# Attention and two mixtures on one core: gates turned by TensorE, next tokens ahead of next weights, rows of the second dense chunk six units later

## The chip, the cores and the metric

The kernel runs on one core of one Trainium2 chip. The metric is the device time of one execution in microseconds (us), lower being better. TensorE does the matmuls (its weight loads are listed apart), VectorE, ScalarE and GpSimd the elementwise work, and SP issues most of the DMAs.

## The reference, cut to what matters

Three stages follow one another; all inputs and the output are float32.

```python
# attention with decay: q, k, v are (4, 8, 576, 64), f is (4, 8, 576)
cum = cumsum(log(clip(f, 1e-4, 1)), -1)
attn = softmax(causal(q @ k^T / 8 + cum[..., :, None] - cum[..., None, :]))
x = heads_side_by_side(attn @ v)                    # 2304 tokens x 512
# one of 8 experts per token (w1: 512 x 1024, w2: 1024 x 512)
logits = unit(x) @ unit(expert_emb).T / tau
e = argmax(logits); gate = softmax(logits)[e]
x = gate * (relu(x @ w1[e]) @ w2[e])
# dense layer for all tokens (w_in: 512 x 2048, w_out: 2048 x 512)
out = softplus(x @ w_in) @ w_out
```

## The kernel before

Every float32 matrix is split into a high part, rounded to the matmul's format, and a low part, the rest; three matmuls (high by high, high by low, low by high) stand for one. ScalarE makes the high part and VectorE (sometimes GpSimd) the low part.

**Attention** (up to about 230 us) computes the 32 heads in pairs and writes the tokens to `xd` in DRAM. **Routing** (`route`, to about 255 us) finds which tokens go to which expert and gives the gather and scatter indices. The change touches neither.

**Experts** (`experts`, L900, about 256 to 545 us) runs nine phases in the order of `ORDER` (L41), each one expert's weights with a block of its tokens: phases 0, 5, 7 and 8 are of kind "t" (three rows of 128 tokens), phases 1 to 4 of kind "b" (two rows), phase 6 of kind "s" (one row). `wide` (L1020) computes the first two kinds, `small` (L1067) the last.

A wide phase has two layers. The first computes eight blocks of 128 hidden features from the turned tokens `xh`, `xl` and the four weight pieces 0 to 3 (`wh`, `wl`; L1037), and ScalarE and VectorE turn each block into `hh`, `hl`. The second (`l2`, L1011, matmuls at L1017) runs over the eight blocks, a unit each: 6 matmuls of 512 columns with two rows, 9 with three, 3 with one. Then `scatter` sends the rows to their places in `yd`.

Between these, the loops issue the work for the next phase:

- `feed` (L964) calls `wsplit` (L943): SP loads one piece of 512 KB into a buffer `raw`, ScalarE writes `wh` (L957), VectorE `wl` (L958). Pieces 4 to 7 of the phase's own second layer come during its first layer, pieces 0 to 3 of the next phase during its second layer. The pool of `raw` has four buffers, which the format conversions of the dense weights (`conv.step`, L1208) share; the table `STEPS` (L38) says at which units those run. A load can start when the VectorE work of the piece four before it has ended.
- `xprep(ph + 1)` (L982) turns the next phase's tokens: for each row four TensorE transposes into a PSUM bank (L994; the pool has two banks), `xh` on ScalarE (L995), `xl` on VectorE (L996). `xgather(ph + 2)` (L972) then gathers the tokens after those through GpSimd's queue.

Each engine executes its instructions in the order in which these calls issue them.

**Gates.** `gates` (L845) is called after phase 0. It computes the gate of every token as `gs`, 128 partitions by 20 columns, five columns for each of the four batches of 576 tokens (four of 128 tokens, one of 64). The dense layer wants `gate` with 18 columns of 128 consecutive tokens. Before, GpSimd's queue writes `gs` to DRAM (`gd`, eight DMAs, L860 and L861) and reads it back (L862), in runs of 4 bytes.

**Dense layer** (`ffn`, L1236, from about 550 us). The 18 rows of 128 tokens form chunks of 4, 3, 4, 3 and 4 rows (`SIZES`); each has 16 units `fb`. A unit's step issues `l1` (12 matmuls, L1293), the softplus on ScalarE, GpSimd (`e`, L1306) and VectorE (result `gh`, `gl`), and the second layer `l2` of the unit three before (L1335). In units 1 to 6 of the first chunk GpSimd also makes the low part of one piece of `w_out` each (L1229). A row of the next chunk is loaded (`yload`, L1260), scaled by its gate on GpSimd and a unit later turned by TensorE and split (`yprep`, L1269); these calls stand at the end of a unit:

```python
for a in range(SIZES[c + 1]):
    if fb == 3 * a:
        yload(c + 1, a)
    if fb == 1 + 3 * a:
        turn = yprep(c + 1, a)
        next(turn)
    if fb == 2 + 3 * a:
        next(turn, None)
```

Of the kernel before, what the change touches and what calls it, by code (L numbers as in the profile page):

```python
# [9 lines left out]
F32 = mybir.dt.float32  # L10
# [14 lines left out]
B, H, S, D = 4, 8, 576, 64  # L25
N = B * S
# [5 lines left out]
T = 5 * B  # L32
# [15 lines left out]
@with_exitstack  # L48
def body(ctx, tc, q, k, v, f, emb, tau, w1, w2, win, wout, out):
    nc = tc.nc  # L50
    const = ctx.enter_context(tc.tile_pool(name="const", bufs=1))
    dram = ctx.enter_context(tc.tile_pool(name="dram", bufs=1, space=DRAM))
    stage = ctx.enter_context(tc.tile_pool(name="stage", bufs=4))
    g = Shared()
    g.stage = stage
    g.xd = dram.tile([N, DM], F32, name="xd")
    g.yd = nc.dram_tensor("yd", [N + 128 * NSLOT, DM], F32, kind="Internal").ap()
    g.ydv = dram_disjoint_views(g.yd, NSLOT)
    g.gd = dram.tile([N, 1], F32, name="gd")
    g.ncum = dram.tile([B * H, S], F32, name="ncum")  # L60

    nc.scalar.preload_act_table_set(LN_EXP)
    g.ident = const.tile([128, 128], F32, name="ident")
    make_identity(nc, g.ident)
    g.gidx = const.tile([128, NMAIN], I32, name="gidx")
    g.sidx = const.tile([128, NMAIN], I32, name="sidx")
    g.ids = const.tile([1, 3 * NG + 4], I32, name="ids")
    g.gate = const.tile([128, N // 128], F32, name="gate")
    g.lt = const.tile([128, T, E], F32, name="lt")
    g.mx = const.tile([128, T, 1], F32, name="mx")  # L70
    g.nrm = const.tile([128, T], F32, name="nrm")
    g.gs = const.tile([128, T], F32, name="gs")
    g.nr = const.tile([128, T, 1], F32, name="nr")

    g.const = const
    g.pre = []
    with ExitStack() as acc:
        ps_s = attention(tc, g, acc, q, k, v, f, emb, tau, w1)
        g.home = ctx.enter_context(tc.tile_pool(name="home", bufs=17, reuse_waits="tile"))
        ring = ctx.enter_context(tc.tile_pool(name="ring", bufs=8, reuse_waits="tile"))  # L80

        def wtile(dt=F32R):
            return (ring.tile([128, 1024], dt, name="wh", tag="wh"), ring.tile([128, 1024], dt, name="wl", tag="wl"))

        g.wtile = wtile
        g.w2a = w2[0]
        with ExitStack() as rtx:
            route(tc, g, rtx.enter_context(tc.tile_pool(name="r_p", bufs=1)), ps_s)
    experts(tc, g, w1, w2, win, wout, out)


# [753 lines left out]
def gates(tc, g):  # L845
    nc = tc.nc
    V = nc.vector
    lt, nr, gs = g.lt, g.nr, g.gs
    nc.scalar.activation(nr[:, :, 0], g.nrm, ACTF.Sqrt)
    nc.scalar.preload_act_table_set(LN_EXP)  # L850
    V.tensor_scalar(nr, nr, 1e-6, None, op0=ALU.add)
    V.reciprocal(nr, nr)
    V.tensor_tensor(lt, lt, g.mx.to_broadcast([128, T, E]), op=ALU.subtract)
    V.tensor_tensor(lt, lt, nr.to_broadcast([128, T, E]), op=ALU.mult)
    nc.scalar.activation(lt, lt, ACTF.Exp)
    V.tensor_reduce(gs, lt, op=ALU.add, axis=AX.X)
    V.tensor_scalar(gs, gs, 1e-9, None, op0=ALU.add)
    V.reciprocal(gs, gs)
    for b in range(B):
        nc.gpsimd.dma_start(g.gd[b * S:b * S + 512, :].rearrange("(r p) o -> p (r o)", p=128), gs[:, 5 * b:5 * b + 4])  # L860
        nc.gpsimd.dma_start(g.gd[b * S + 512:b * S + S, :], gs[0:64, 5 * b + 4:5 * b + 5])  # L861
    nc.gpsimd.dma_start(g.gate, g.gd.rearrange("(t p) o -> p (t o)", p=128))  # L862


def tail_slots(tc, g, p, psp, scratch, M):
# [34 lines left out]
def experts(tc, g, w1, w2, win, wout, out):  # L900
# [6 lines left out]
    with ExitStack() as ctx:  # L907
# [112 lines left out]
        def wide(ph):  # L1020
# [30 lines left out]
            for i, (rows, fb) in enumerate([([a], fb) for a in range(w) for fb in range(8)] if last else  # L1051
                                           [(list(range(w)), fb) for fb in range(8)]):
                l2(ph, py, hts[fb], fb, rows)
                if i == 2:
                    xprep(ph + 1)
                    xgather(ph + 2)
                if not last:
                    feed(ph, min(i + 1, 4))
                if not last and STEPS[ph][8 + i]:
                    conv.step()  # L1060
                if last and i % 3 == 1:
# [5 lines left out]
        def small(ph, after1=None):  # L1067
# [48 lines left out]
            py = [ps_y.tile([128, DM], F32, name="y", tag="y")]  # L1116
            for fb in range(8):
                l2(ph, py, hts[fb], fb, [0])
                if fb == 1 and not after1:
                    hts += turn(h1)  # L1120
                if fb == 3 and main:
                    xprep(ph + 1)
                    xgather(ph + 2)
                if fb < 4:
                    next_weights(fb + 1)
            scatter(ph, 0, py[0])
# [54 lines left out]
        xgather(1)  # L1181
        for c in range(4, 8):
            wsplit(0, c)
        for ph in range(n_ph):
            (small if phases[ph][0] == "s" else wide)(ph)
            W.pop(ph)
# [49 lines left out]
def ffn(tc, g, conv, out):  # L1236
# [6 lines left out]
    with ExitStack() as ctx:  # L1243
# [111 lines left out]
        for n in range(len(units) + 3):  # L1355
# [15 lines left out]
            if n >= 3:  # L1371
                l2(*units[n - 3])
            if n < len(units) and c + 1 < NC:
                for a in range(SIZES[c + 1]):
                    if fb == 3 * a:
                        yload(c + 1, a)
                    if fb == 1 + 3 * a:
                        turn = yprep(c + 1, a)
                        next(turn)
                    if fb == 2 + 3 * a:  # L1380
                        next(turn, None)


# [33 lines left out]
```

## Time and profile before

| | |
|---|---|
| three runs | 983.41, 978.90 and 975.82 us, median 978.9 |
| profiled execution | 976.53 us, of which the span from first to last instruction is 974.4 |
| mean granted clock of TensorE | 0.963 of full speed |
| busy | TensorE 889.7 us, its weight loads 760.5, VectorE 616.5, ScalarE 604.3, GpSimd 352.5 |

Rows of the trace give a start in us from the beginning of the span, a duration in us, the engine, the line, the operation, what it writes and reads, and in square brackets the idle time before it with the instruction or DMA that ended it. PE is TensorE, DVE VectorE, ACT ScalarE, POOL GpSimd, SPq the DMA issues of SP. A row may stand for several instructions (x2). Ends of matmuls are modelled, so the distance of starts is the better measure of them.

### The profile page before, as it was taken

To read this page: it belongs to the slowest core of one execution; us is meant where nothing else is said; L and a number is where in the kernel's file an instruction comes from. 1 tells how busy PE (TensorE), PEld (TensorE's weight loads), DVE (VectorE), ACT (ScalarE), POOL (GpSimd) and SP (SyncE) were. 2 spreads that over 40 slices of the span, in tenths; PEclk is the share of its full clock that TensorE was granted. 3 is DMA by queue.
4 is the path that set the end of the run, shared out by engine and by line. 5 is a ranking of instruction groups with operands and counts; after the bars stand their busy time and mean duration, and the time that the engine had idled before them with its cause. 6 is when DMAs were issued, how large, how long until landed. Compare 5 with 4: busy or idle time off the path is not lost. (4 is left out here: it accounts for less than half of the span.)

```text
span 974.4 us, 17371 instructions
## 1 busy us (share of the span) xinstructions
PE 889.7 (91%) x6292; PEld 760.5 (78%) x6292; DVE 616.5 (63%) x1321; ACT 604.3 (62%) x1139; POOL 352.5 (36%) x479
## 2 busy tenths in 40 slices
PE   3999999998199599899899579999999999999998
PEld 2788887887199489797788468889988888998886
DVE  3888888887676367666669547455546455555444
ACT  4778888786525255544435367667677666767664
POOL 6776786773403112111101047223323222322221
PEclk9999999999599889999899789999999999999999
DMA  8766665741537887777764200001001001000001
GB/s 182 170 156 150 159 162 141 209 105 37 209 102 195 143 282 271 268 239 246 246 222 162 89 12 12 11 1 66 23 1 54 11 1 54 23 1 33 1 0 44
DMA packets 103327, 109.41 MB, mean 112 GB/s; under 512 B 62584, under 2 KB 71800, under 8 KB 103232
## 3 DMA queue, kind: packets, MB, share of 16 engines
q1 hardware_dynamic: 99296, 97.02, 35.4%
q0 software_dynamic: 3680, 11.03, 3.3%
q8 instruction: 51, 0.84, 0.4%
q14 instruction: 44, 0.36, 0.1%
q10 hardware_dynamic: 256, 0.16, 0.1%
HBM read 93.16 MB, written 15.03 MB: 111 GB/s over the span
## 5 line engine op out<-in xcount | busy, mean ns | idle before, releaser
L1323 DVE TENSOR_TENSOR gl<-e,gh 128x512 fp32r<-128x512 f32 (+1 forms) x80 | 99.2, 1239 | 178.0 <-ACT gh L1321 178.0
L1306 POOL TENSOR_TENSOR e<-u,e 128x512 f32<-128x512 f32 (+1 forms) x80 | 94.6, 1182 | 291.4 <-ACT u L1305 271.4
L1293 PE MATMUL h<-yth,dl 128*128 128x512 f32 (+1 forms) x320 | 119.0, 372 | 0.0
L1302 ACT ACTIVATE e<-h 128x512 f32<-128x512 f32 (+1 forms) x80 | 44.4, 556 | 113.5 <-PE h L1293 94.8
L1335 PE MATMUL o<-dl,gh 128*128 128x512 f32 x288 | 112.5, 391 | 0.0
L958 DVE TENSOR_TENSOR wl<-raw,wh 128x1024 fp32r<-128x1024 f32 x64 | 77.7, 1223 | 33.3 <-ACT wh L957 32.7
L957 ACT ACTIVATE wh<-raw 128x1024 fp32r<-128x1024 f32 x64 | 66.7, 1056 | 38.0 <-DMA raw<-in_moe_w_dram 37.3
L1037 PE MATMUL h<-xh,wh 128*128 128x384 f32 (+1 forms) x256 | 81.7, 319 | 8.4 <-ACT xh L995 6.9
L1037 PE MATMUL h<-xl,wh 128*128 128x384 f32 (+1 forms) x256 | 81.1, 317 | 2.7 <-DVE xl L996 2.7
L1037 PE MATMUL h<-xh,wl 128*128 128x384 f32 (+1 forms) x256 | 80.8, 316 | 0.5 <-issue 0.5
L320 DVE SCALAR_TENSOR_TENSOR pts<-pt,pts 128x512 f16<-128x512 f32 (+3 forms) x128 | 69.8, 567 | 11.9 <-ACT pts L317 11.2
L317 ACT ACTIVATE pts<-pt 128x512 f16<-128x512 f32 (+3 forms) x128 | 58.4, 495 | 22.1 <-PE pt L330 10.6
L294 ACT ACTIVATE p<-sm,mx 128x512 f32<-128x512 f32 (+3 forms) x128 | 67.8, 558 | 0.0
L1017 PE MATMUL y<-wh,hh 128*128 128x512 f32 x168 | 67.5, 402 | 0.0
L1017 PE MATMUL y<-wl,hh 128*128 128x512 f32 x168 | 66.4, 395 | 0.8 <-DVE wl L958 0.8
L1293 PEld LDWEIGHTS h<-yth,dl 128*128 128x128 f32 x320 | 60.8, 190 | 7.8
L291 DVE CUSTOM_DVE_ANT_0 sm<-s,cb 128x512 f32<-128x512 f32 (+3 forms) x128 | 58.3, 484 | 8.0 <-PE s L271 7.1
L1008 POOL DMA_INDIRECT yd<-y,sidx x21 | 21.2, 1007 | 115.9 <-ACT y L1001 112.9
L978 POOL DMA_INDIRECT xg<-xd,gidx x21 | 24.6, 1169 | 105.7 <-PE xt L994 95.8
L1318 DVE TENSOR_TENSOR e<-e,v 128x512 f32<-128x512 f32 (+1 forms) x80 | 57.5, 718 | 7.7 <-DVE e L1317 0.5
L1335 PEld LDWEIGHTS o<-dl,gh 128*128 128x128 f32 x288 | 54.1, 188 | 10.3
L1293 PE MATMUL h<-yth,wh 128*128 128x512 f32 (+1 forms) x160 | 61.5, 384 | 0.7 <-ACT yth L1281 0.7
(294 smaller groups left out, 2606.2 us busy)
## 6 DMA issues: line engine op xcount, KB each, us to landing
raw<-in_moe_w_dram SPq DMA_DIRECT2D x68, 512.0 KB, 4.5
cb<-ncum SPq DMA_DIRECT2D x32, 288.0 KB, 4.8
raw<-in_moe_w_in_dram SPq DMA_DIRECT2D x16, 512.0 KB, 5.7
raw<-in_moe_w_out_dram SPq DMA_DIRECT2D x16, 512.0 KB, 3.9
cb<-ncum SPq DMA_DIRECT2D x32, 144.0 KB, 4.5
out_dram<-ob SPq DMA_DIRECT2D x18, 256.0 KB, 2.4
qt<-in_q_dram SPq DMA_DIRECT2D x32, 128.0 KB, 2.6
kt<-in_k_dram SPq DMA_DIRECT2D x32, 128.0 KB, 2.5
```

The lines of the kernel that those rows point to most:

```text
L291: nc.vector.tensor_tensor_reduce(out=s[:, 0:n], in0=ps[h][:, 0:n], in1=c[:, h, 0:n], scale=-0.125, scalar=1e30, op0=ALU.add, op1=ALU.min, ...
L294: nc.scalar.activation(p[:, 0:n], s[:, 0:n], ACTF.Exp, scale=-1.0, bias=m)
L317: nc.scalar.activation(hi, ps, ACTF.Copy, scale=UP)
L320: nc.vector.scalar_tensor_tensor(lo, ps, UP, hi, op0=ALU.mult, op1=ALU.subtract)
L957: nc.scalar.activation(hi, r, ACTF.Copy)
L958: nc.vector.tensor_sub(lo, r, hi.bitcast(F32))
L1017: nc.tensor.matmul(py[a], x[:, 128 * a:128 * a + 128], w[:, fb % 2], start=(fb == 0 and m == 0 and w is wh), stop=(fb == 7 and m == 1))
L1037: nc.tensor.matmul(pl, x[:, fs], y[:, c], start=(c == 0 and m == 0), stop=(c == 3 and m == 2))
L1293: nc.tensor.matmul(pl, w[:, fs], x[:, d], start=(d == 0 and m == 0), stop=(d == 3 and m == 2))
L1306: nc.gpsimd.tensor_sub(e, u, e)
L1323: nc.vector.tensor_sub(gl, d, gh.bitcast(F32))
L1335: nc.tensor.matmul(PO[c][a], x, w, start=(fb == 0 and m == 0 and w is wh), stop=(fb == FB - 1 and m == 1))
```

## The change

Three edits. The gates are turned on the core: a first transpose gives 20 x 128, VectorE swaps its two halves of 64, a second transpose turns it back, and four copies put the pieces in place. The two transposes stand after units 5 and 6 of phase 1's second layer. In a phase's second layer, `xprep` and `xgather` come after the first unit (before: after the third in `wide`, the fourth in `small`), and in `wide` the pieces of the next weights come one unit later; in `small` the turn of the second hidden half comes after the first unit too (before: the second). In the dense layer, the three rows of the second chunk are loaded and turned in units 6 to 14 of the first, before in 0 to 8.

```diff
-    for b in range(B):
-        nc.gpsimd.dma_start(g.gd[b * S:b * S + 512, :].rearrange("(r p) o -> p (r o)", p=128), gs[:, 5 * b:5 * b + 4])
-        nc.gpsimd.dma_start(g.gd[b * S + 512:b * S + S, :], gs[0:64, 5 * b + 4:5 * b + 5])
-    nc.gpsimd.dma_start(g.gate, g.gd.rearrange("(t p) o -> p (t o)", p=128))
+def turn_gates(tc, g, p, psp):
+    nc = tc.nc
+    V = nc.vector
+    t = psp.tile([128, 128], F32, name="gt", tag="T")
+    nc.tensor.transpose(t[0:T], g.gs, g.ident)
+    turned = p.tile([T, 2, 64], F32, name="turned", bufs=1)
+    for x in range(2):
+        V.tensor_copy(turned[:, x], t[0:T, 64 - 64 * x:128 - 64 * x])
+    yield
+    t = psp.tile([128, 128], F32, name="gt", tag="T")
+    nc.tensor.transpose(t[:, 0:T], turned.rearrange("p x n -> p (x n)"), g.ident[0:T, 0:T])
+    to = g.gate.rearrange("p (b t) -> p b t", b=2)
+    here = g.gs.rearrange("p (b x t) -> p b x t", b=2, x=2)[:, :, 0]
+    there = t[:, 0:T].rearrange("p (b x t) -> p b x t", b=2, x=2)[:, :, 1]
+    V.tensor_copy(to[:, :, 0:4], here[:, :, 0:4])
+    V.tensor_copy(to[0:64, :, 4:5], here[0:64, :, 4:5])
+    V.tensor_copy(to[64:128, :, 4:9], there[64:128])
+    V.tensor_copy(to[0:64, :, 5:9], there[0:64, :, 0:4])
...
@@ wide
-                if i == 2:
+                if i == 0:
                     xprep(ph + 1)
                     xgather(ph + 2)
-                if not last:
-                    feed(ph, min(i + 1, 4))
+                elif not last:
+                    feed(ph, min(i, 4))
+                if ph == 1 and i in (5, 6):
+                    next(turned, None)
                 if not last and STEPS[ph][8 + i]:
                     conv.step()
...
@@ small
-                if fb == 1 and not after1:
+                if fb == 0 and not after1:
                     hts += turn(h1)
-                if fb == 3 and main:
-                    xprep(ph + 1)
-                    xgather(ph + 2)
+                    if main:
+                        xprep(ph + 1)
+                        xgather(ph + 2)
...
@@ ffn
+                x = 0 if c else 6
                 for a in range(SIZES[c + 1]):
-                    if fb == 3 * a:
+                    if fb == x + 3 * a:
                         yload(c + 1, a)
...
```

Three places of the order show what moves. First VectorE in phase 1, from the end of its first layer to the first block of phase 2; `wl` are weight splits, `xl` the next tokens, `dw` a format conversion, `hl` the phase's hidden features. Before:

```order
L958 TENSOR_TENSOR wl<-raw,wh 128x1024 x3
L1220 TENSOR_SCALAR dw<-raw 128x512
L1221 SCALAR_TENSOR_TENSOR dw<-raw,dw 128x512
L1222 SCALAR_TENSOR_TENSOR dw<-raw,dw 128x512
L996 TENSOR_TENSOR xl<-xt,xh 128x4x128 x2
L958 TENSOR_TENSOR wl<-raw,wh 128x1024 x2
L1043 SCALAR_TENSOR_TENSOR hl<-h,hh 128x512
```

The same place now, with `turned` and `gate` as the copies of the gates:

```order
L973 TENSOR_TENSOR wl<-raw,wh 128x1024
L1011 TENSOR_TENSOR xl<-xt,xh 128x4x128 x2
L973 TENSOR_TENSOR wl<-raw,wh 128x1024
L1238 TENSOR_SCALAR dw<-raw 128x512
L1239 SCALAR_TENSOR_TENSOR dw<-raw,dw 128x512
L1240 SCALAR_TENSOR_TENSOR dw<-raw,dw 128x512
L973 TENSOR_TENSOR wl<-raw,wh 128x1024 x3
L867 COPY turned<-gt 20x64 x2
L874 COPY gate<-gs 128x2x4
L875 COPY gate<-gs 64x2
L876 COPY gate<-gt 64x2x5
L877 COPY gate<-gt 64x2x4
```

The two `xl` moved from behind the first two pieces of the next weights to ahead of them, the conversion from behind the second piece to ahead of it, and the six copies stand behind all four pieces.

Next ScalarE in phase 6, the small one; `hs` are its hidden features before the turn, `hh<-ht` after it, `xh` the tokens of phase 7. Before:

```order
L1079 ACTIVATE hs<-h 128x512
L957 ACTIVATE wh<-raw 128x1024 x2
L1088 ACTIVATE hh<-ht 128x512
L957 ACTIVATE wh<-raw 128x1024 x2
L995 ACTIVATE xh<-xt 128x4x128 x3
L957 ACTIVATE wh<-raw 128x1024
L1001 ACTIVATE y<-y 128x512
```

And now:

```order
L1096 ACTIVATE hs<-h 128x512
L972 ACTIVATE wh<-raw 128x1024
L1105 ACTIVATE hh<-ht 128x512
L1010 ACTIVATE xh<-xt 128x4x128 x3
L972 ACTIVATE wh<-raw 128x1024 x4
L1016 ACTIVATE y<-y 128x512
```

Three pieces of phase 7's weights stood ahead of its tokens; now all four stand behind them.

Last GpSimd at the start of the dense layer; `e` is a step of the softplus, `dl` the low part of a piece of `w_out`, `yg` the scaling of a row of the second chunk. Before:

```order
L1306 TENSOR_TENSOR e<-u,e 128x512 x2
L1229 TENSOR_TENSOR dl<-dw,wh 128x1024
L1276 TENSOR_SCALAR yg<-yg,gate 128x512
L1306 TENSOR_TENSOR e<-u,e 128x512
L1229 TENSOR_TENSOR dl<-dw,wl 128x1024
```

And now, from the sixth of the six `dl` on:

```order
L1247 TENSOR_TENSOR dl<-dw,wl 128x1024
L1324 TENSOR_TENSOR e<-u,e 128x512
L1294 TENSOR_SCALAR yg<-yg,gate 128x512
L1324 TENSOR_TENSOR e<-u,e 128x512 x3
L1294 TENSOR_SCALAR yg<-yg,gate 128x512
```

The first scaling moved from behind the first `dl` to behind the last.

## Rows read from the trace of the kernel before

**Rows 1.** The page: busy shares (part 1) and DMA issues (part 6)

```profile
PE 889.7 (91%) x6292; PEld 760.5 (78%) x6292; DVE 616.5 (63%) x1321; ACT 604.3 (62%) x1139; POOL 352.5 (36%) x479
...
raw<-in_moe_w_dram SPq DMA_DIRECT2D x68, 512.0 KB, 4.5
```

**Rows 2.** Timeline of TensorE, where the layers of phases 1 to 3 begin

```profile
316.09 0.40 PE L1017 MATMUL y<-wh,hh 128*128 128x512 f32 x1
...
336.29 0.58 PE L1037 MATMUL h<-xh,wh 128*128 128x256 f32 x1 [6.91 <-ACT xh L995]
...
339.57 0.58 PE L1037 MATMUL h<-xl,wh 128*128 128x256 f32 x1 [2.70 <-DVE xl L996]
...
355.01 0.40 PE L1017 MATMUL y<-wh,hh 128*128 128x512 f32 x1
...
366.81 0.28 PE L1037 MATMUL h<-xh,wh 128*128 128x256 f32 x1
...
378.32 0.40 PE L1017 MATMUL y<-wh,hh 128*128 128x512 f32 x1
```

**Rows 3.** Timeline of ScalarE and GpSimd, 324 to 337 us

```profile
324.22 1.06 ACT L957 ACTIVATE wh<-raw 128x1024 fp32r<-128x1024 f32 x1 [7.27 <-DMA raw<-in_moe_w_dram]
332.92 1.06 ACT L957 ACTIVATE wh<-raw 128x1024 fp32r<-128x1024 f32 x1 [7.64 <-DMA raw<-in_moe_w_dram]
...
333.71 1.26 POOL L862 DMA_DIRECT2D gate<-gd  x1 [17.92 <-DMA gd<-gs]
...
335.17 1.07 ACT L995 ACTIVATE xh<-xt 128x512 fp32r<-128x512 f32 x2
```

**Rows 4.** Windows: busy PE, PEld, DVE, ACT, POOL, granted clock, DMA share, GB/s

```profile
310.00:315.00 5.00, 5.00 (x44) 5.00 (x43) 4.61 (x7) 3.67 (x5) 4.75 (x7) 1.00 0.94 38
...
335.00:340.00 5.00, 1.01 (x3) 0.71 (x4) 4.87 (x8) 2.27 (x4) 2.12 (x2) 0.50 0.72 144
...
405.00:410.00 5.00, 1.81 (x13) 1.36 (x11) 4.41 (x7) 2.15 (x3) 1.77 (x1) 1.00 0.89 293
...
465.00:470.00 5.00, 1.87 (x7) 1.68 (x8) 3.16 (x5) 2.75 (x5) 0.84 (x2) 0.65 0.99 378
```

**Rows 5.** Timeline of TensorE and VectorE before phases 5 and 7

```profile
403.45 2.36 DVE L958 TENSOR_TENSOR wl<-raw,wh 128x1024 fp32r<-128x1024 f32 x2 [0.26 <-ACT wh L957]
...
410.00 0.66 PE L994 MATMUL xt<-ident,xg 128*128 128x128 f32 x4 [3.19 <-DVE xl L996]
...
411.33 0.69 DVE L996 TENSOR_TENSOR xl<-xt,xh 128x512 fp32r<-128x512 f32 x1 [0.78 <-ACT xh L995]
...
458.80 2.35 DVE L958 TENSOR_TENSOR wl<-raw,wh 128x1024 fp32r<-128x1024 f32 x2
...
468.13 1.11 PE L994 MATMUL xt<-ident,xg 128*128 128x128 f32 x4 [4.02 <-DVE xl L996]
...
473.77 0.33 PE L1037 MATMUL h<-xh,wh 128*128 128x384 f32 x1
```

**Rows 6.** Timeline of VectorE, GpSimd and TensorE at the dense layer's start

```profile
569.71 1.34 DVE L1323 TENSOR_TENSOR gl<-e,gh 128x512 fp32r<-128x512 f32 x1 [0.79 <-ACT gh L1321]
...
573.23 1.14 POOL L1276 TENSOR_SCALAR yg<-yg,gate 128x512 f32<-128x512 f32 x1
...
574.42 1.11 PE L1280 MATMUL yt<-ident,yg 128*128 128x128 f32 x4 [5.60 <-POOL yg L1276]
...
579.84 0.39 PE L1335 MATMUL o<-wh,gh 128*128 128x512 f32 x1
```

**Rows 7.** Timeline of SP, ScalarE and VectorE, the last loads before phase 3

```profile
358.04 1.47 SPq L935 DMA_DIRECT2D raw<-in_moe_w_dram  x2
...
364.23 1.06 ACT L957 ACTIVATE wh<-raw 128x1024 fp32r<-128x1024 f32 x1 [1.77 <-DMA raw<-in_moe_w_dram]
...
365.33 1.23 DVE L958 TENSOR_TENSOR wl<-raw,wh 128x1024 fp32r<-128x1024 f32 x1 [0.93 <-ACT wh L957]
```

**Rows 8.** The chain that ended last: one piece of the dense layer

```profile
582.75 2.72 PE h L1293 x12
```

More of the change, by code (lines that the diff above doesn't have):

```diff
@@ L58, in body @@
     g.ydv = dram_disjoint_views(g.yd, NSLOT)
-    g.gd = dram.tile([N, 1], F32, name="gd")
     g.ncum = dram.tile([B * H, S], F32, name="ncum")
@@ L1183, in experts @@
             wsplit(0, c)
+        turned = turn_gates(tc, g, hp, ps_t)
         for ph in range(n_ph):
@@ L1373, in ffn @@
             if n < len(units) and c + 1 < NC:
+                x = 0 if c else 6
                 for a in range(SIZES[c + 1]):
-                    if fb == 3 * a:
+                    if fb == x + 3 * a:
                         yload(c + 1, a)
-                    if fb == 1 + 3 * a:
+                    if fb == x + 1 + 3 * a:
                         turn = yprep(c + 1, a)
                         next(turn)
-                    if fb == 2 + 3 * a:
+                    if fb == x + 2 + 3 * a:
                         next(turn, None)
```

## The prediction

> **What bounds the kernel now.** I read the busy shares first: TensorE is busy for 91% of the span [rows 1], so only its idle time and its half-clock time can be won. Then I listed TensorE's gaps from 250 us on. Four stretches matter here; the reader should see in each which engine's row ends last.
>
> (1) The border from expert phase 1 to phase 2. Phase 1's second-layer run begins at 316.09, phase 2's first layer at 336.29, its second layer at 355.01, a distance of 38.92 us; for phases 2 to 3, of the same shape, it is 378.32 - 355.01 = 23.31 [rows 2]. So 15.6 us are lost. ScalarE waits 7.27 and then 7.64 us for weight loads to land before it can reach the two token splits `xh` at 335.17 [rows 3]. Such a load lands after 4.5 us in the median [rows 1]. In those microseconds the gate DMAs of GpSimd are under way: their read-back waited 17.92 us for the writes [rows 3], and from 310 to 315 the DMA engines are busy for 0.94 of the time at 38 GB/s [rows 4]. Then TensorE starts cold: 335 to 340 at granted clock 0.50, the 1.2 GHz level [rows 4].
>
> (2) and (3) The borders into three-row phases. The third row's transposes need a PSUM bank that the first row's `xl` frees, and `xl` stands behind weight splits: TensorE waits 3.19 us at 410.00 and 4.02 us at 468.13 [rows 5].
>
> (4) The dense layer. After its third unit TensorE waits 5.60 us for GpSimd's scaling of a row of chunk 1, which runs at 573.23 without a pause before it: GpSimd was busy with weight splits [rows 6].
>
> **The change part by part.**
>
> *Gates.* Nine DMAs go; GpSimd has nothing to wait for there, and the loads behind 310 us should land in the usual 4.5 us. If everything then runs as from phase 2 to 3, the 15.6 us come back. What is added is a wait. The second gate transpose stands before the last unit of phase 1's second layer and needs two copies on VectorE, which stand behind all four `wl` of the next weights. From phase 2 to 3 the last load (the second of two issued from 358.04) is in use by ScalarE at 364.23 and its `wl` ends at 365.33 + 1.23 = 366.56; the next phase starts at 366.81 [rows 2, 7]. Twelve matmuls of 512 columns take 2.72 us at full clock [rows 8], so a unit of two rows (six) takes 1.36, eight of them 10.9 of the 11.80 us of phase 2's second layer, and the eight transposes of the two rows the other 0.9. The gate transpose would want its data at 366.81 - 1.36 = 365.45. The two `xl` now run ahead of `wl` 0, whose end frees the buffer for the last load, so that load comes 2 x 0.69 = 1.4 us later (the width of 411.33 in rows 5); two copies, each far under the 0.69 us of a 512-column `xl`, take some 0.3. The wait: 366.56 + 1.4 + 0.3 - 365.45 = 2.8 us. Its bounds are 0.3 (copies alone) and 7.6 (the longest weight wait in rows 3). I take 2.8 and 0.1 for the transposes: **12.7 us won**, between 8 and 15.3. Behind the waiting transpose stand six matmuls and then phase 2, which needs the same `wl` 1.1 us after its start anyway.
>
> A 3.19 us wait left the clock at 1.00 (405 to 410); after the 4.02 us wait it was 0.65 (465 to 470) [rows 4, 5]. So I cost 2.8 us without a clock loss. The Trainium skill (TensorE: Matmul & The Clock Gate, "What's actually happening") says that the half rate is the default and only activity lifts it; a longer wait would then cost twice, which is a rival below.
>
> *Tokens ahead of weights.* Into phase 5 the second row's transposes ended at 410.00 - 3.19 = 406.81; two units earlier is 404.09. VectorE's pair of `wl` from 403.45 is the last of the current phase and the first of the next; after the first of them, at 404.65, `xl` comes now, and ends at 405.34 [rows 5]. The third row waits 1.3 us instead of 3.19: **1.9 us won** (0 to 3.2). Into phase 7 the last two `wl` of the small phase end at 458.80 + 2.35 = 461.15; then come the split of the second hidden half, as wide as an `xl`, at 461.84, and the first `xl` at 462.53, for which the third row waits [rows 5]. With 0.45 for its transposes and seven units of 0.68 us (three matmuls), phase 7 starts at 467.7, not 473.77: **6.0 us won** (2 to 8; below that only if the loads of its weights land later than now). The other borders show no such wait, and gain nothing.
>
> The price is later weights. At a start with 1.33 us in hand (`wl` 3 ends 366.56, needed three quarters of a 1.44 us unit after 366.81) `wl` 3 now comes 1.4 us later, so the slack is just used up: cost 0, at most 1 us at each of two starts (2 to 3, 3 to 4). On SP the format conversion's load moves ahead of load 1, not of loads 2 and 3. Borders out of three-row phases have longer units that cover the shift.
>
> *Rows of chunk 1.* TensorE ended the third unit at 574.42 - 5.60 = 568.82. The fourth unit's 12 matmuls (2.72 us) then end at 571.54, and the second-layer run that began at 579.84 can begin there: its data `gl` ends at 569.71 + 1.34 = 571.05 [rows 6, 8]. 8.3 us minus 0.4 for the transposes' new place: **7.9 us won** (5.6, the wait alone, to 8.3). In units 6 to 14 GpSimd has no split left (six, one each in units 1 to 6), which covers the scaling.
>
> **Sum.** 12.7 + 1.9 + 6.0 + 7.9 = 28.5 us. The profiled execution took 976.5 us (span 974.4), hence 948.0; it lies 2.4 us under the median of the three runs, so I forecast **950.4 us** against 978.9.
>
> By one page the sum would be another. The Trainium skill (DMA: Bandwidth & Descriptors, "Anatomy of one DMA") gives a DMA of this kind some 2 us plus its bytes at 436 GB/s; nine DMAs of at most 9 KB would then disturb nobody, and the first term would vanish. The 17.92 us wait of rows 3 is against that.
>
> **Rivals.**
>
> *The gate DMAs are not the jam.* Then the loads stay slow, and the new wait comes on top at its upper bound, since nothing of phase 2 can run before it: 976.5 + 7.6 - 1.9 - 6.0 - 7.9 = 968.3, as a median 970.7. For it: the slow loads go on after the writes are issued. Against it: rate and wait change with the first gate DMA. Chance 0.06.
>
> *The gate wait is long.* After a wait like the 4.02 us one the clock is down [rows 4, 5]. At 6 us of wait plus the 4.5 us by which phase 2's cold first layer exceeded a warm one (355.01 - 336.29 = 18.72, minus 2.70 of wait, minus 378.32 - 366.81 = 11.51) [rows 2], the first term is 15.6 - 6 - 4.5 = 5.1, the total 20.9, the time 958.0. For it: the copies stand behind the last load. Chance 0.15.
>
> *No gate wait.* Loads land sooner than I credit, and `wl` 3 is through in time: the first term is 15.3, the time 947.8. Against it: rows 7 leave 1.1 us too little even before the shift. Chance 0.11.
>
> *Slower: weights late at every start.* The shift works back through the four load buffers; place: the first unit of seven phases; price: a wait of 4 us and as much again for the half clock, 7 x 8 = 56 us, minus 28.5: 1006. It decides once each of the seven starts waits as long as phase 7's turn did, that is if a load took some 9 us to land in undisturbed phases. For it: the slack is used up as worked out above. Against it: loads land in 4.5. Chance 0.04.
>
> **How the numbers follow.** The forecast holds 0.64; its own range, with the terms some halfway to their bounds, is 944 to 956. To leave out no more than two tenths, the range is 943 to 962: it takes in the long gate wait and the missing one. A measurement of this kernel tells about 1% (10 us) from no change. Faster by more than that: the forecast and both gate-wait cases, 0.90; within 1%: the first rival, 0.06; slower: 0.04.
>
> **What would show it.** Right: no ScalarE wait over 3 us for weight loads in phase 1; phase 2's second layer some 26 us after phase 1's; a TensorE wait of 2 to 4 us at the second gate transpose; waits of about 1.3 us at three-row turns; no wait of the dense layer's fourth unit. Wrong: weight loads in phase 1 landing after 10 us; new waits at the first unit of phases 2 to 4; a granted clock of 0.5 after the gate transpose; the dense layer waiting for `gl` instead of the row.

## The result and the profile after

The changed kernel takes 952.7 us (median of four runs, 951.77 to 954.28), the kernel before 978.25 in the runs beside it (975.82 to 983.41): a ratio of 0.9734, with a 95% interval from 0.9692 to 0.9776. The forecast was 950.4, its range 943 to 962.

The profiled execution of the changed kernel took 951.77 us, its span 949.7, against 976.53 and 974.4 before: 24.7 us won. Cut at the starts of layers on TensorE, the two spans compare like this ("layer 1" and "layer 2" are the two layers of an expert phase):

| piece of the span | before | after | won |
|---|---|---|---|
| start to phase 1, layer 1 | 304.58 | 305.55 | -0.97 |
| to phase 2, layer 2 | 50.43 | 37.32 | 13.11 |
| to phase 4, layer 2 | 46.66 | 46.66 | 0 |
| to phase 5, layer 1 | 15.66 | 13.70 | 1.96 |
| to phase 6, layer 2 | 40.04 | 40.20 | -0.16 |
| to phase 7, layer 2 | 33.04 | 28.38 | 4.66 |
| to phase 8, layer 2 | 37.29 | 37.39 | -0.10 |
| to the first dense matmul | 30.95 | 31.87 | -0.92 |
| to the first dense second-layer run | 21.19 | 13.81 | 7.38 |
| to the end | 394.56 | 394.82 | -0.26 |

These are the rows of TensorE behind it. The first group answers to [rows 2], 393.19 and 447.86 to the three-row turns of [rows 5], the last two to the dense start of [rows 6]. A row gives start, duration, engine, line, operation, out<-in and, in brackets, the idle time before it and what ended it.

```profile
317.06 0.40 PE L1032 MATMUL y<-wh,hh 128*128 128x512 f32 x1
329.72 0.20 PE L870 MATMUL gt<-ident,turned 20*128 20x20 f32 x1 [1.91 <-DVE turned L867]
331.36 0.28 PE L1052 MATMUL h<-xh,wh 128*128 128x256 f32 x1
342.87 0.40 PE L1032 MATMUL y<-wh,hh 128*128 128x512 f32 x1
354.68 0.28 PE L1052 MATMUL h<-xh,wh 128*128 128x256 f32 x1
366.18 0.40 PE L1032 MATMUL y<-wh,hh 128*128 128x512 f32 x1
...
393.19 0.66 PE L1009 MATMUL xt<-ident,xg 128*128 128x128 f32 x4 [1.23 <-DVE xl L1011]
...
447.86 1.97 PE L1009 MATMUL xt<-ident,xg 128*128 128x128 f32 x8 [1.50 <-DVE hl L1106]
455.14 0.33 PE L1052 MATMUL h<-xh,wh 128*128 128x384 f32 x1
471.81 0.39 PE L1032 MATMUL y<-wh,hh 128*128 128x512 f32 x1
...
541.07 0.79 PE L1311 MATMUL h<-yth,wh 128*128 128x512 f32 x1 [0.69 <-ACT yth L1299]
554.88 0.39 PE L1353 MATMUL o<-wh,gh 128*128 128x512 f32 x1
```

The page's first part has TensorE busy for 93% of the span, where it was 91% [rows 1]:

```profile
PE 884.3 (93%) x6294; PEld 758.0 (80%) x6294; DVE 617.4 (65%) x1327; ACT 604.8 (64%) x1139; POOL 345.6 (36%) x470
```

From 317.06 to 342.87 it is now 25.81 us where it was 38.92, and the next border, 342.87 to 366.18, is the 23.31 it was before. Of the 2.50 us that still part the two, 1.91 are the wait for `turned`, the copies that stand between the two gate transposes; the other 0.6 were not followed up.

ScalarE's timeline in the same stretch answers to [rows 3]. Its waits for weight loads were 7.27 and 7.64 us; these three are now the ones that are left.

```profile
323.01 1.06 ACT L972 ACTIVATE wh<-raw 128x1024 fp32r<-128x1024 f32 x1 [1.82 <-DMA raw<-in_moe_w_dram]
325.50 1.06 ACT L972 ACTIVATE wh<-raw 128x1024 fp32r<-128x1024 f32 x1 [1.43 <-DMA raw<-in_moe_w_dram]
327.00 1.06 ACT L972 ACTIVATE wh<-raw 128x1024 fp32r<-128x1024 f32 x1 [0.45 <-DMA raw<-in_moe_w_dram]
```

The windows answer to [rows 4]; the last three numbers are the granted clock, the DMA engines' busy share and GB/s.

```profile
310.00:315.00 5.00, 5.00 (x44) 5.00 (x43) 4.41 (x9) 3.70 (x7) 0.98 (x1) 1.00 0.47 152
325.00:330.00 5.00, 3.09 (x15) 2.17 (x14) 3.27 (x8) 2.12 (x2) 0.00 (x0) 1.00 0.94 325
335.00:340.00 5.00, 5.00 (x44) 5.00 (x44) 3.90 (x6) 2.52 (x4) 0.84 (x1) 1.00 0.63 210
...
445.00:450.00 5.00, 3.50 (x18) 3.15 (x19) 3.76 (x5) 2.58 (x5) 2.17 (x2) 0.78 0.86 270
...
540.00:545.00 5.00, 4.31 (x11) 2.81 (x10) 1.25 (x2) 0.60 (x1) 0.00 (x0) 0.50 0.02 3
```

310 to 315 was 38 GB/s at a busy share of 0.94 and is 152 at 0.47. 335 to 340 is at full clock. Two of the stretches in the table run at a lower one: phase 6 from 445 on, and the first dense units from 540 on.

### The profile page after: what moved, and what is told of

Read it like the earlier page. It is cut to its first block, busy times and chain, and to the rows that moved or that the text cites. A ratio compares the mean times of both kernels' runs of the same rounds, so it can differ in the third digit from the quotient of the medians.

```text
span 949.7 us, 17374 instructions
## 1 busy us (share of the span) xinstructions
PE 884.3 (93%) x6294; PEld 758.0 (80%) x6294; DVE 617.4 (65%) x1327; ACT 604.8 (64%) x1139; POOL 345.6 (36%) x470
## 4 chain that ended last, share of the span: by engine, by line
PE 76%; DMA 7%; issue 6%; ACT 5%; DVE 4%; POOL 1%; SPq 0%; DVEq 0%; ACTq 0%; POOLq 0%
PE h L1311 21%; PE o L1353 21%; PE y L1032 7%; PE h L1052 6%; DMA yd<-y,sidx 4%; PE s L268 4%; PE av L391 2%; PE pt L339 2%; PE tps L195 2%; DVE wl L973 1%; PE av L392 1%; PE av L393 1%; PE s L270 1%; PE s L274 1%; DMA raw<-in_moe_w_dram 1%
## 5 line engine op out<-in xcount | busy, mean ns | idle before, releaser
L316 ACT ACTIVATE pts<-pt 128x512 f16<-128x512 f32 (+3 forms) x128 | 58.3, 495 | 22.6 <-PE pt L339 10.9
L1336 DVE TENSOR_TENSOR e<-e,v 128x512 f32<-128x512 f32 (+1 forms) x80 | 59.8, 747 | 7.4
L391 PE MATMUL av<-vp,pts 128*128 128x65 f16 (+2 forms) x480 | 59.2, 197 | 0.5 <-DVE vbits L240 0.5
```

What stands on the lines that cost most here:

```text
L391: nc.tensor.matmul(o, ph, vp[0:kk, j, h, 0:D + 1], start=(j == 0), stop=False)
L1336: nc.vector.tensor_add(d, d, u)
```

## The experiments

Three theories stood open. The gate DMAs may have jammed the weight loads, or merely have stood beside slow loads. The order of tokens and weights may pay by the missing waits, or be eaten by later weights. The dense units may have lost their 5.6 us wait, or wait elsewhere.

### One edit alone, three times

The kernel before with the first edit of the change only (the diff of `gates` and `turn_gates`):

> The kernel before with the first edit alone: gates turned by TensorE after units 5 and 6 of phase 1, no gate DMAs, everything else in the old order. Theory (the 4-byte gate DMAs held up the weight loads): from the second layer of phase 1 to that of phase 2 about 14 us less than before, one more than in the changed kernel, because in the old order the last weight piece comes about 1.3 us earlier and the second gate transpose waits some 0.6 us instead of 1.91; time about 964 us. Rival (the slow border came from the order, tokens behind weights, and the DMAs only happened beside it): ScalarE still waits over 7 us for weight loads, and the gain stays under 4 us, 975 us or more.

The kernel before with the second edit only (`i == 2` to `i == 0`, `feed` one unit later, and `small`):

> The kernel before with the second edit alone: tokens ahead of the next weights, gate DMAs kept. Theory: the border out of phase 1 stays slow, since its loads land late whatever the order (0 to 1 us won); 2 us are won before phase 5 and 4.7 before phase 7 as in the changed kernel; time about 971 us. Rival (the order is the main part of the change): the border out of phase 1 shrinks by 8 us or more, and the time falls to 963 or less.

The kernel before with the third edit only (`x = 0 if c else 6`):

> The kernel before with the third edit alone: rows of the second dense chunk six units later. Theory: no TensorE wait for a scaled row in the dense layer's fourth unit, 7 to 8 us from the first dense matmul to the first second-layer run; time about 971 us. Rival (the softplus chain of ScalarE and VectorE would have held the fourth unit anyway): a wait for the softplus takes the place of the 5.6 us, and the gain is under 3 us.

Measured, beside a kernel before of 980.34 us in these runs:

| | median us | ratio (95%) |
|---|---|---|
| gates only | 964.25 | 0.9847 (0.9816 to 0.9877) |
| order only | 972.6 | 0.9924 (0.9900 to 0.9948) |
| dense only | 973.12 | 0.9916 (0.9886 to 0.9945) |

16.1, 7.7 and 7.2 us: each edit pays by itself. The sum, 31.0, lies 5.5 above the whole (978.25 - 952.7 = 25.6), but the kernel before was slower beside these runs than beside those of the result; a second set of runs of the changed kernel, below, gives 27.0 for the whole (980.02 - 953.03). With intervals of 2.4 to 4 us to either side of each of the four, no interaction can be told from this. The stretch from phase 1, layer 1 to phase 2, layer 2 is 37.31 us with the gates alone, as in the changed kernel:

```profile
305.60 0.28 PE L1052 MATMUL h<-xh,wh 128*128 128x256 f32 x1
...
329.77 0.20 PE L870 MATMUL gt<-ident,turned 20*128 20x20 f32 x1 [1.88 <-DVE turned L867]
...
342.91 0.40 PE L1032 MATMUL y<-wh,hh 128*128 128x512 f32 x1
```

So the gate wait stands there with the old order of tokens too, and is not the 0.6 us that were expected of it; it does not come from the tokens' being ahead. With the order alone the gate DMAs stay, and their stretch is 51.64 us, no better than the 50.43 of before. Its rows at phase 7, from the second layer of phase 6 to that of phase 7, are taken up further down:

```profile
460.42 0.51 PE L1017 MATMUL y<-wh,hh 128*128 128x512 f32 x1
470.74 0.33 PE L1037 MATMUL h<-xh,wh 128*128 128x384 f32 x1
...
488.31 0.39 PE L1017 MATMUL y<-wh,hh 128*128 128x512 f32 x1
```

With the dense edit alone the first dense second-layer run comes 12.68 us after the first matmul, before 21.19: 8.5 us less. 8.3 were forecast for this stretch, of which 0.4 were to be paid later.

### The gate DMAs put back, three ways

The changed kernel with DMAs added behind the gates, none of whose data is used. First the nine old ones (the lines that set up the buffers are left out here and below):

```diff
...
+    for b in range(B):
+        nc.gpsimd.dma_start(g.gd[b * S:b * S + 512, :].rearrange("(r p) o -> p (r o)", p=128), gs[:, 5 * b:5 * b + 4])
+        nc.gpsimd.dma_start(g.gd[b * S + 512:b * S + S, :], gs[0:64, 5 * b + 4:5 * b + 5])
+    nc.gpsimd.dma_start(g.spare[:, 0:18], g.gd.rearrange("(t p) o -> p (t o)", p=128))
```

> The changed kernel with the nine old gate DMAs back at their old place, but into a spare buffer that nothing reads: 2304 values written and read in runs of 4 bytes. Theory (those DMAs take the DMA engines from the weight loads): weight loads issued in phase 1 land 10 us late and more, the second gate transpose waits 10 us or more behind the last piece, the clock falls, and the time is 10 to 20 us longer than the changed kernel's, 963 to 973 us. Rival (only GpSimd's waiting for them cost time, nothing waits for GpSimd now): within 2 us of the changed kernel.

Then the eight writes without the last line:

> The changed kernel with the eight old gate writes to DRAM in runs of 4 bytes, without the read back. If the writes jam the loads by themselves: ScalarE's first wait for a load in phase 1 is 7 to 9 us as with all nine, the second one is 4 us or less because the read back is missing, and the time is 960 to 966. If writes and read share the price otherwise: either 968 or more (the writes alone do it all), or within 3 us of 952.7 (the read alone does it).

And nine DMAs that move more bytes in longer runs:

```diff
...
+    for r in g.gds:
+        nc.gpsimd.dma_start(r, gs)
+    nc.gpsimd.dma_start(g.spare, g.gds[7])
```

> The changed kernel with nine extra GpSimd DMAs at the place of the old gate DMAs: eight writes of the whole tile gs (128 runs of 80 bytes each) and one read back in such runs, into a spare tile that nobody reads. Theory (the jam comes of the 4-byte runs): weight loads of phase 1 keep landing in about 4.5 us, the second gate transpose waits 1.5 to 4 us, the time is within 3 us of the changed kernel's 952.7. Rival (any nine DMAs through GpSimd's queue jam the loads): as in the run with the nine old DMAs, 968 to 973, with a ScalarE wait of 7 us or more for a load in phase 1.

| | median us | phase 1, layer 1 to phase 2, layer 2 | second gate transpose waits |
|---|---|---|---|
| changed kernel | 952.7 | 37.32 | 1.91 |
| nine DMAs, runs of 80 bytes | 955.44 | 40.92 | 4.00 |
| eight writes, runs of 4 bytes | 966.79 | 51.57 | 11.41 |
| writes and read, runs of 4 bytes | 971.06 | 56.31 | 16.09 |

ScalarE and GpSimd with all nine old DMAs:

```profile
325.91 1.06 ACT L978 ACTIVATE wh<-raw 128x1024 fp32r<-128x1024 f32 x1 [8.14 <-DMA raw<-in_moe_w_dram]
336.25 1.06 ACT L978 ACTIVATE wh<-raw 128x1024 fp32r<-128x1024 f32 x1 [8.31 <-DMA raw<-in_moe_w_dram]
...
337.18 1.26 POOL L863 DMA_DIRECT2D spare<-gd  x1 [20.58 <-DMA gd<-gs]
```

With the eight writes alone:

```profile
325.15 1.06 ACT L977 ACTIVATE wh<-raw 128x1024 fp32r<-128x1024 f32 x1 [7.53 <-DMA raw<-in_moe_w_dram]
332.92 1.06 ACT L977 ACTIVATE wh<-raw 128x1024 fp32r<-128x1024 f32 x1 [5.74 <-DMA raw<-in_moe_w_dram]
```

With the runs of 80 bytes:

```profile
328.42 1.06 ACT L977 ACTIVATE wh<-raw 128x1024 fp32r<-128x1024 f32 x1 [2.03 <-DMA raw<-in_moe_w_dram]
...
319.62 0.54 POOL L862 DMA_DIRECT2D spare<-gd  x1 [4.55 <-DMA gd<-gs]
```

That settles that the gate DMAs were the jam. As many DMAs of longer runs cost 2.7 us, the old ones 18.4, and of these the writes alone 14.1. Each of the eight longer writes carries the whole tile, 10 KB, more than all eight old ones together (2304 gates of 4 bytes, 9 KB), and they land sooner. These are the DMA issues of the page (KB each, median us from issue to landing), first for the eight old writes, then for the eight longer ones:

```profile
gd<-gs POOLq DMA_DIRECT2D x4, 2.0 KB, 12.9
gd<-gs POOLq DMA_DIRECT2D x4, 0.2 KB, 15.3
...
gd<-gs POOLq DMA_DIRECT2D x8, 10.0 KB, 3.2
```

So neither the count of DMAs nor the bytes make the jam; the short runs do. Their length and their number changed together (2304 runs of 4 bytes, 1024 of 80), and no run parts these two.

The 18.4 us are not the price of the DMAs alone. Order only has the same nine DMAs and no gate transpose, and its stretch is 51.64 us, not 56.31. The 4.7 us between them go with the second gate transpose: it waits 16.09 us for copies that stand behind the last piece of weights, while phase 2 by itself can begin with the pieces that are there. That is read from the two profiles; no run shows it apart. Of the text on the writes alone one part fell: ScalarE's second wait was 5.74 us, not 4 or less, so that the read adds less than was thought, 4.3 us.

### The second gate transpose moved into phase 2

The new place lies three second-layer units and the whole first layer of phase 2 behind the old one; "two units later" counts too few.

```diff
-                if ph == 1 and i in (5, 6):
+                if (ph, i) in ((1, 5), (2, 1)):
```

> The changed kernel with the second gate transpose two units later, after the second unit of phase 2's second layer, where the turned halves are long there. Theory (the transpose's wait of 1.91 us is on the path, nothing behind it waits for the same weights): phase 1's second layer to phase 2's second layer takes 35.4 us instead of 37.3, the time is 1.9 us less, about 950.8. Rival (phase 2's first layer would wait for the same last piece of weights anyway): the wait moves to that piece and the distance stays within 0.5 us of 37.3.

949.78 us (947.77 to 952.42), ratio 0.9698 (0.9671 to 0.9725). From 306.90 to 341.90 the stretch is 35.00 us, 2.3 less than in the changed kernel, and the transpose waits for nothing:

```profile
318.41 0.40 PE L1032 MATMUL y<-wh,hh 128*128 128x512 f32 x1
330.39 0.28 PE L1052 MATMUL h<-xh,wh 128*128 128x256 f32 x1
341.90 0.40 PE L1032 MATMUL y<-wh,hh 128*128 128x512 f32 x1
345.65 0.23 PE L870 MATMUL gt<-ident,turned 20*128 20x20 f32 x1
...
379.94 0.39 PE L1052 MATMUL h<-xh,wl 128*128 128x256 f32 x1 [0.76 <-DVE wl L973]
```

The wait was on the path, all of it; phase 2 does not wait for the same piece of weights in its place. 0.4 us of the gain go at the next border: from phase 2's second layer to phase 3 it is 12.20 us, 11.81 in the changed kernel. The last row is something else: a wait for `wl` at the start of phase 4, which the runs below take up.

### Units between the rows of phase 7

```diff
...
                 if fb == 0 and not after1:
                     hts += turn(h1)
                     if main:
-                        xprep(ph + 1)
-                        xgather(ph + 2)
-                if fb < 4:
+                        rest = xrows(ph + 1)
+                        next(rest, None)
+                if fb == 2 and main:
+                    for _ in rest:
+                        pass
+                    xgather(ph + 2)
+                if 2 <= fb < 4:
                     next_weights(fb + 1)
```

> The changed kernel with phase 6 in another order: after its first second-layer unit come the turn of the second hidden half and the first of phase 7's token rows, then two units, then the other two rows; the weight splits that stood behind the first two units come after the third. Theory: TensorE's wait of 1.50 us for a PSUM bank is filled with the two units (1.36 us), the clock stays at 1.00 in phase 6, and VectorE's four weight splits become what phase 7 waits for: phase 6's second layer to phase 7's takes 1.4 to 3 us less than the 28.4 us it takes now, the time is 950 to 951.5. Rival (VectorE bounds this border already): the same wait turns up in phase 7's first units and the distance stays within 0.7 us.

952.59 us, the changed kernel's time. The idle 1.50 us are filled and phase 7 begins 8.95 us after phase 6's second layer instead of 11.71, and then it waits:

```profile
445.61 0.50 PE L1037 MATMUL y<-wh,hh 128*128 128x512 f32 x1
454.56 0.33 PE L1057 MATMUL h<-xh,wh 128*128 128x384 f32 x1
...
458.65 0.69 PE L1057 MATMUL h<-xh,wl 128*128 128x384 f32 x1 [0.64 <-DVE wl L973]
...
475.05 0.39 PE L1037 MATMUL y<-wh,hh 128*128 128x512 f32 x1
```

Layer 2 to layer 2 is 29.44 us, 1.06 more than in the changed kernel. The theory fell. What phase 7 waits for now are its weights, in three waits of 0.33, 0.48 and 0.64 us, with the clock at 0.79 from 460 to 465; that is the rival's mechanism, though the distance grew by more than its 0.7 us. The edit itself put the first two of these splits up to two units later, so the run does not show that they bounded the border before it.

### The changed kernel again, and matmuls ahead of the dense layer

> The changed kernel once more, unchanged. In the first profile the clock fell in phase 6 behind the waits of 0.83 and 1.50 us and phase 4's first layer took 11.52 us; in the other kernels with the same code there (the nine scratch DMAs, the later second transpose) the same waits left the clock at 1.00, and phase 4's first layer took 12.7 to 12.8 us. If both belong to the single execution and not to the kernel: the time is again 951 to 955, and at least one of the two comes out the other way here. If they belong to the kernel: phase 6 shows half clock again and phase 4 takes 11.5.

```diff
...
+        for t, idle in zip(turns, (20, 0, 4, 0)):
+            for _ in range(idle):
+                nc.tensor.matmul(bank.rearrange("p a n -> p (a n)"), w[:, 0:128], x, start=True, stop=True)
             next(t, None)
```

> The changed kernel with 24 matmuls of 512 columns added that nobody reads, on pieces of w_in that are ready by then: 20 ahead of the first transposes of the dense layer's tokens, 4 between the second and the third row. They stand where TensorE waits some 9 and some 1 us. Theory (the dense term came out 0.9 us short because the first units ran at the lower clock level, which follows from the idle time ahead of them): the granted clock is 1.00 in the first units, the first dense matmul to the first second-layer run takes 10.9 us instead of 13.81, and the time is 2 to 4 us less than the changed kernel's, 949 to 951. Rival (the first units wait for data too, or the added matmuls run at half clock and delay the transposes): the distance stays above 12.5 us or the first dense matmul comes later by what is won, and the time is 952 or more.

The changed kernel again: 953.03 us (951.88 to 955.07). Phase 4's first layer took 12.18 us this time, not 11.52; the clock fell in phase 6 again (450 to 455 at 0.66), and this time also behind the gate wait. Two of its windows:

```profile
330.00:335.00 5.00, 4.31 (x18) 3.89 (x19) 1.02 (x7) 1.08 (x2) 1.13 (x2) 0.67 0.65 221
450.00:455.00 5.00, 3.98 (x15) 3.51 (x16) 3.46 (x6) 2.90 (x5) 3.14 (x3) 0.66 0.79 277
```

So phase 4's late weights belong to the execution. For phase 6 this run could not decide alone; the ten profiles together do (below).

With the added matmuls: 951.56 us (950.23 to 954.04). They run partly at half clock, and from 535 us on the clock is 1.00; the dense units begin warm:

```profile
530.00:535.00 5.00, 4.62 (x13) 3.70 (x14) 2.45 (x2) 2.01 (x2) 0.17 (x1) 0.66 0.21 61
535.00:540.00 5.00, 3.95 (x20) 2.61 (x18) 1.46 (x3) 1.19 (x2) 0.00 (x0) 1.00 0.75 257
540.00:545.00 5.00, 3.54 (x17) 2.49 (x18) 2.97 (x5) 1.19 (x2) 0.00 (x0) 1.00 0.02 5
```

The first dense matmul to the first second-layer run is 11.50 us (542.52 to 554.02), 2.3 less than the 13.81, where 10.9 was expected: the second matmul still waits for `ytl`. Without the added matmuls the eight profiles with the third edit have 12.68 to 13.98 us there, so a part of the 2.3 may belong to the execution; with them the three profiles have 11.50, 11.52 and 12.82 us (the last two are those of the next section). In the median that leaves 1.5 us against the same kernel without them, inside the spread of both; that the clock can be held up is shown in the profile, the gain in time is not settled by these four runs.

### Two versions put together

The later transpose with the added matmuls:

> The changed kernel with the second gate transpose after the second unit of phase 2's second layer and with the 24 added matmuls ahead of the dense layer. If both gains stand side by side: 1.9 to 2.4 us for the first and 2 to 4 for the second, together 946 to 949.

The same, with the early tokens only ahead of phases of three rows:

```diff
...
-                if i == 0:
+                early = not last and WIDTH[phases[ph + 1][0]] == 3
+                if i == (0 if early else 2):
                     xprep(ph + 1)
                     xgather(ph + 2)
-                elif not last:
-                    feed(ph, min(i, 4))
+                if not last and not (early and i == 0):
+                    feed(ph, min(i if early else i + 1, 4))
```

> As the run before, with the tokens ahead of the next weights only where the next phase has three rows (into phases 5, 7 and 8); elsewhere the old order, tokens after the third unit. Theory (the new order pays at the borders into three-row phases only, and costs at the start of phase 4, where the last piece of weights comes late): phase 4's first layer takes 11.5 us in every execution instead of 11.5 to 13.9, and the time is 0 to 2 us below that of the run before, 945 to 948. Rival (the early tokens are worth something at the two-row borders too): a new wait at the start of phases 2 to 4 or 6, and 949 or more.

948.97 us (946.03 to 950.37) for the first, at the upper end of what was expected. In its profile the added matmuls did not hold the clock: it was 0.66 from 540 to 545, and the first dense units took 12.82 us. The second takes 947.41 us (946.11 to 949.69), ratio 0.9675 (0.9643 to 0.9707). All six of its runs lie below all eight of the changed kernel, whose fastest is 951.77: it beats both kernels, by some 5 and some 32 us. That it beats the first by 1.6 us is not settled, since their runs overlap. Its profile shows what was asked:

```profile
346.34 0.63 PE L1009 MATMUL xt<-ident,xg 128*128 128x128 f32 x4 [0.78 <-PE xt L1009]
...
376.94 0.28 PE L1052 MATMUL h<-xh,wh 128*128 128x256 f32 x1
...
388.46 0.40 PE L1032 MATMUL y<-wh,hh 128*128 128x512 f32 x1
```

Phase 4's first layer is 11.52 us, as in the kernels with the old order (before, gates only and dense only: 11.51 to 11.52). In the ten profiles with the new order there (order only, and the changed kernel with all its other versions) it is 11.52, 11.77, 11.81, 12.07, 12.18, 12.53, 12.73, 12.83, 13.18 and 13.86. Part of it is given back earlier: phase 2's second layer to phase 3 is 13.17 us, where the first version has 12.20. TensorE waits 0.78 us there between the two rows' transposes, behind the gate transpose, which now stands ahead of the tokens. Likely the gate transpose is the reason; no run parts the two.

## Why the prediction was right, and where it was off

**What bounds the kernel.** Right. In the four stretches the named rows ended last: each edit by itself moved its own stretches by what it moves them in the changed kernel, or more.

**Gates: 12.7 us predicted, 13.11 measured.** The mechanism is shown by putting the DMAs back, the size by the edit alone (13.12 in the profile, 50.43 to 37.31). That the number came so close is in part luck. The gate wait was put at 2.8 us, "without a clock loss"; with the transpose in that place five profiles show 1.88, 1.91, 1.91, 2.65 and 2.85. The working behind the 2.8 held less well than its size: the load that "comes 1.4 us later" behind the tokens did not make it, since with the old order the wait is 1.88.

The step "I cost 2.8 us without a clock loss" failed at the size it was made for. In the three profiles with the shorter waits the clock stays at 1.00, and the stretch without its wait is 35.4 us (37.32 - 1.91, and the like). In the two with the longer ones it falls: behind 2.65 us in the second profile of the changed kernel (first row; 0.67 from 330 to 335, above), and behind 2.85 us in the one with the added matmuls.

```profile
330.69 0.20 PE L870 MATMUL gt<-ident,turned 20*128 20x20 f32 x1 [2.65 <-DVE turned L867]
...
329.30 0.26 PE L870 MATMUL gt<-ident,turned 20*128 20x20 f32 x1 [2.85 <-DVE turned L867]
330.00:335.00 5.00, 5.00 (x28) 4.43 (x27) 0.00 (x0) 1.09 (x2) 1.74 (x2) 0.73 0.54 168
```

There the stretch without its wait is 36.9 us (39.57 - 2.65 and 39.76 - 2.85): 1.5 us go to the clock, and the term is 10.9 and 10.7 us instead of 13.1. That is the rival of the long wait in a small size, 1.5 us of its 4.5. The runs of 80 bytes show the same 1.5 us behind their 4.00 us wait (40.92 - 4.00 = 36.9).

**The page on DMAs.** From the figures of the Trainium skill (DMA: Bandwidth & Descriptors, "Anatomy of one DMA"), some 2 us and the bytes at 436 GB/s, the prediction estimated that the nine DMAs would disturb nobody. The runs decide against that for runs of 4 bytes (18.4 us with all that follows from them), and come near to it for runs of 80 bytes (2.7 us).

**Tokens ahead into phase 5: 1.9 predicted, 1.96 measured**, with a wait of 1.23 us where 1.3 was worked out.

**Tokens ahead into phase 7: 6.0 predicted, 4.66 measured.** This term was mis-sized. The start itself was placed rightly: where the clock stays at 1.00, it comes 10.32 us after phase 6's second layer (order only), 6.1 less than the 16.40 of before. TensorE's wait stands one row earlier than was worked out: it is the second row that waits 1.50 us, for the `hl` of the second hidden half, and not the third for `xl`.

Two steps were not priced. The seven units were taken at full clock; in the changed kernel two short waits, 0.83 and 1.50 us, are followed by half clock, and the start comes 11.71 us after. Phase 7's first layer then takes as long as before (16.67 us), so 4.66 us are left. And where the clock stays up and the start does come early, phase 7's weights are late: in order only its first layer takes 17.57 us instead of 16.64, with a wait of 0.20 us for `wl` among others, and 5.15 us are left. The other three profiles with the clock at 1.00 have 17.56 to 17.85 us. So one cost hides most of the other: the ten profiles with this order into phase 7 (all but the one with units between its rows) win 3.9 to 5.2 us, none the 6.0. The units put between the rows filled the idle time at the price of later weights, and won nothing.

**Late weights at the other starts: 0 predicted, at most 1 each.** 0 at phase 3 (its first layer is 11.50 us in the changed kernel); at phase 4 from 0 to 2.3 us (11.52 to 13.86 us for the layer). The slack was indeed "just used up", so it falls to one side or the other from one execution to the next, and the upper bound of 1 was too low. The waits at the first units of phases 2 to 4 that were named as a sign of being wrong did come, at phase 4 and in a small size.

**Dense rows: 7.9 predicted, 7.1 measured** (7.38 - 0.26); 8.5 before the later cost in the edit alone. The 5.60 us wait is gone and no other took its place. What is missing is clock, which the prediction took over from the profile before: there too the first dense units began at 0.50, but the clock was at 0.80 from 561.45 to 562.85 and at 1.00 from there, 4.2 us after the first matmul. In the changed kernel it is at 0.50 until 5.6 us after it. That differs from one execution to the next (12.68 to 13.98 us for the stretch in eight profiles, above). Matmuls ahead of these units brought it to 11.5 us in two profiles of three.

**The sum: 28.5 predicted, 24.7 between the two profiles.** The four terms make 26.85 (13.11 + 1.96 + 4.66 + 7.12), and 2.15 are lost elsewhere. The forecast of the median is off by less, 952.7 against 950.4: it added 2.4 us for the distance of the profiled execution from the median, and in the changed kernel that distance is 0.9. This part is luck.

**Not in the sum:** 0.97 us lost before phase 1 and 0.92 ahead of the dense layer, both in code that the change leaves alone. The second is the third row of tokens, which landed late (VectorE waited 2.17 us for it); over the profiles of the experiments the same wait is 0.22 to 1.76 us. The start of phase 1 lies between 304.18 and 306.90 us in them. So both look like what one execution differs from the next.

## What to carry to other kernels

Small transfers in runs of 4 bytes can cost most where they were not issued: here the weight loads beside them came late. Turn such data on the core, and look for the jam in windows of much DMA busy time at few GB/s (0.94 at 38 GB/s here). When work is moved ahead of something with just enough slack, price that slack as a spread, not as zero, and follow the gain to the next layer's start but one: it may be won at the first and lost at the second. Price a new wait of TensorE at both clocks: of the waits at the gate transpose those of 1.88 and 1.91 us cost themselves alone, those of 2.65, 2.85 and 4.00 us each 1.5 us besides. A wait that an edit adds in front of one instruction can be taken off the path by moving that instruction behind work that has its data; here that won 2.3 us of the stretch.

## What was not expected of the hardware

The same pair of waits in phase 6 (0.83 and 1.49 or 1.50 us, the same instructions around them) lowered the granted clock in six of ten profiles (0.77 to 0.80 in the mean from the end of the second wait to phase 7, the border 11.53 to 11.80 us) and left it at 1.00 in four (10.32 or 10.33 us). Here is the one with the second transpose later, where it stayed:

```profile
445.00:450.00 5.00, 3.29 (x21) 2.66 (x22) 4.22 (x6) 3.29 (x7) 2.38 (x2) 1.00 0.91 297
```

So the length of a wait alone does not tell whether the clock falls: before, 3.19 us left it at 1.00 [rows 4, 5]; here 2.3 us in two pieces did not, in six cases of ten. The Trainium skill (TensorE: Matmul & The Clock Gate, "What's actually happening") says that the activity is watched over a window that runs freely beside the program, and that the moment of the change depends on where in it the first matmul lands. By that, the place of the waits in it would decide; six of ten does not speak against it, and no run here moved the waits alone to show it.

SP issues ahead of the units that call for its loads. The first row of the second chunk is called for six units later in the changed kernel, and its load is still issued right behind the first four:

```profile
531.35 1.89 SPq L1284 DMA_DIRECT2D y<-yd  x4
533.28 0.43 SPq L1284 DMA_DIRECT2D yg<-yd  x1
```

What moved was the use of the row, on GpSimd and TensorE. Here an issue that had nothing to wait for did not move with the unit it is written in.
